# New ranks and engine allowances for all work from the second batch's keys on

## The chip, the cores and the metric

The kernel runs on one core of a Trainium2 chip. TensorE (PE; PEld is its weight load) does the matmuls, VectorE (DVE), ScalarE (ACT) and GpSimd (POOL) the elementwise work, and SyncE (SP) issues every DMA from one queue. Each engine works through its own instruction stream strictly in the order in which it was written and waits on semaphores of the others. The metric is the device time of one execution in microseconds, lower is better.

## The reference

Three layers over 4 batches of 576 tokens, in fp32:

```python
# attention: 8 heads of 64; heads 0-3 see the last 32 keys, heads 4-7 every 4th of the last 128
scores = np.where(mask, q @ k.T / 8, -1e9)
attn = np.exp(scores - max); attn = attn / (attn.sum() + 1e-9)
x = attn @ v                                    # (4, 576, 512)
# first feed-forward: x_prev is x shifted by one token
xk = mu_k * x + (1 - mu_k) * x_prev;  xr = mu_r * x + (1 - mu_r) * x_prev
k = np.maximum(xk @ w_k, 0);  v = k * k @ w_v   # w_k (512, 1024), w_v (1024, 512)
x = 1 / (1 + np.exp(-(xr @ w_r))) * v
# second: gated, with a mix over the tokens
h = np.maximum(x @ w_in, 0);  u, v = h[..., :512], h[..., 512:]
v_n = (v - mean(v)) / sqrt(var(v) + 1e-6)
v_s = einsum('ts,bsd->btd', w_spatial, v_n) + b_spatial[:, None]
out = (u * v_s) @ w_out
```

## The kernel before

**Numbers.** A product of two fp32 matrices is done as three matmuls in a faster type: each operand is split into a high part (a copy that rounds, on ACT or DVE) and a low part (a subtraction, on DVE or POOL). So every operand costs one copy and one subtraction before TensorE can read it. The function `halves` records both.

**Names.** Work is recorded in steps with a tag of step, batch and, where there are two, half: `ld` loads queries and keys (16 small DMAs for a half of the heads), `qk` turns them on DVE (tiles `qT`, `kT`), `vw` loads values (10 or 12 DMAs), `soft` is scores (`psS`), mask and maximum (`pr`, `mx`), exponential, sum and division (`sm`, `st`, `pr`), transposition on TensorE (`psT`) and copy (`pt`); `val` multiplies by the values and copies to `x`. `k` (mixed input `xd`, `xm`, `xh`, `xl`; after the matmul `kr`, then squares split into `kh`, `kl`, shown in profiles as `sq_dt`), `r` and `v` are the first feed-forward; `s` splits its successor's weights. In the second layer `x2`, `u2`, `v2`, `vn` do the input product by a seven-product scheme over 2 by 2 blocks; `V` splits the normalised half (tiles `V`, `VS`, `wt`), `sp` is the mix over tokens (sums in `R` or `wf`; the gated product is split into `gh`, `gl`), `out` the last product (`ot`, then the store).

**The order.** Nothing is issued while the steps are recorded. The class `Plan` keeps for each operation its dependencies, its engines with a cost in ns for each, and a base rank. At the end `Plan.order` plays a greedy schedule forward: whenever an engine is free, it takes, of the operations that are ready by the plan's own clock, the one with the lowest rank. If an operation may run on more than one engine, an engine takes it only when no other would end it sooner, each end counted with an allowance in ns that is added for DVE and POOL (ACT has none). The engines' instruction streams are then written in that order. The rank and the allowances come from the table `TUNE`; `k / count` runs from 0 to just under 1 over the operations of one kind in a step:

```python
more, grow, dve_, pool_ = TUNE.get(g[0], {}).get(g[1], (0, 0, 792, 22))
prio.append(o[5] + more + grow * (k / count[g]))
self.pens.append({"dve": dve_, "pool": pool_})
...
free[e] = start + (460 if e == "dma" else cost[e])
...
def dve(n):
    return 70 + n * 1.042
```

The base rank is about 1000 per half batch in the first layer (2825 and 3611 for the attention of batch 2), 10000 to 13500 in the second. Up to 100 us the plan also fills TensorE's idle time with matmuls on constants. Two tiles hold loaded queries and keys and two hold values, so a load can start only when its tile's last reader is done; the DMAs stand in SP's queue in the planned order, and one that waits holds up all behind it.

**Which order results.** Attention of a batch runs among the first feed-forward of the batch before it. The second layer begins near 320 us. Its last part, `V`, `sp` and `out` for the batches in the order 2, 3, 0, 1, begins near 455 us.

Of the kernel before, what the change touches and what calls it, by code (L numbers as in the profile page):

```python
# [36 lines left out]
def blocks(dil):  # L37
# [40 lines left out]
    ('out', 0): {'ot': (-48481, 1635, 400, -300), 'out': (-15787, -1962, 400, 2000), 'psB': (-26874, 3252, 200, 0)},  # L78
    ('out', 1): {'ot': (11033, 6529, 1500, 300), 'out': (81304, 27, 400, -800), 'psB': (60486, 11220, 1500, 2000)},
    ('out', 2): {'ot': (-40922, 4560, 792, -300), 'out': (29151, 33499, 200, -800), 'psB': (42562, 2655, 200, 22)},  # L80
    ('out', 3): {'ot': (-54092, -274, 200, 2000), 'out': (-39436, 37850, 200, -800), 'psB': (-39698, 3601, 200, 300)},
# [33 lines left out]
    ('spill', 0): {'spill': (-77802, 20888, 200, 2000)},  # L115
    ('spill', 1): {'spill': (7310, -4425, 1500, 800)},
    ('start',): {'ident': (5243, -7493, 792, 22), 'identb': (-2035, 973, 792, 22), 'mask': (0, 0, 792, 22), 'mask2': (0, 0, 792, 22), 'pt': (7412, 207, 792, 800), 'xok': (11235, 2251, 792, 22)},
    ('tail',): {'ed': (19937, 5909, -200, 800), 'eh': (19594, -4924, -600, 300), 'el': (26278, 3273, -200, 300), 'wt': (42392, -29077, 792, 2000)},
    ('tailu', 0): {'psB': (-49671, 13322, 1500, 0), 'utl': (-90359, -26564, 400, -800)},
# [2209 lines left out]
```

## Time and profile before

| | |
|---|---|
| median of 3 runs | 587.37 us (587.1 to 587.73) |
| the profiled execution's own time | 584.21 us |
| its span, first to last instruction | 582.4 us |
| PE busy | 556.1 us, 95% |
| DVE busy | 450.9 us, 77% |
| ACT busy | 300.4 us, 52% |
| POOL busy | 197.0 us, 34% |
| mean granted TensorE clock | 0.992 |

The profile is one execution; times inside it are counted from the span's start. Busy time of PE is the union of its matmuls, which are pipelined, so short stalls between them do not show as idle. The helper class that records the program gives nearly all instructions the same line, so they are told apart by their tiles.

### The profile page before, as it was taken

To read this page: it belongs to the slowest core of one execution; us is meant where nothing else is said; L and a number is where in the kernel's file an instruction comes from. 1 tells how busy PE (TensorE), PEld (TensorE's weight loads), DVE (VectorE), ACT (ScalarE), POOL (GpSimd) and SP (SyncE) were. 2 spreads that over 40 slices of the span, in tenths; PEclk is the share of its full clock that TensorE was granted. 3 is DMA by queue.
4 is the path that set the end of the run, shared out by engine and by line. 5 is a ranking of instruction groups with operands and counts; after the bars stand their busy time and mean duration, and the time that the engine had idled before them with its cause. 6 is when DMAs were issued, how large, how long until landed. Compare 5 with 4: busy or idle time off the path is not lost.

```text
span 582.4 us, 14108 instructions
## 1 busy us (share of the span) xinstructions
PE 556.1 (95%) x5714; PEld 517.8 (89%) x5715; DVE 450.9 (77%) x904; ACT 300.4 (52%) x734; POOL 197.0 (34%) x210
## 2 busy tenths in 40 slices
PE   8889999997989999999999999999999998899996
PEld 7767798796979999999999999999999998689885
DVE  7689998887979464554279984799989999976960
ACT  4579977785244271354738563364442466442231
POOL 1023402721144012122323501237664256573610
PEclk9899999999989999999999999999999999999999
DMA  9889572436656102000024120021010041311012
GB/s 243 243 204 217 146 187 48 77 95 129 105 129 121 19 29 65 1 2 1 1 73 146 52 62 1 26 59 73 1 74 2 1 181 36 109 73 55 2 73 91
DMA packets 91521, 47.35 MB, mean 81 GB/s; under 512 B 77184, under 2 KB 83328, under 8 KB 90944
## 3 DMA queue, kind: packets, MB, share of 16 engines
q1 hardware_dynamic: 91456, 46.45, 31.0%
q8 instruction: 45, 0.74, 0.5%
q14 instruction: 20, 0.16, 0.1%
HBM read 39.62 MB, written 6.82 MB: 80 GB/s over the span
## 4 chain that ended last, share of the span: by engine, by line
PE 66%; DVE 22%; ACT 5%; issue 3%; DMA 1%; POOL 1%; SPq 1%; DVEq 0%; ACTq 0%; POOLq 0%
PE psM L463 41%; PE psB L463 16%; PE psT L463 6%; DVE R L463 3%; PE psS L463 2%; DVE wf L463 2%; DVE num L463 2%; DVE x L463 1%; DVE V L463 1%; DVE VS L463 1%; DVE pt L463 1%; SPq L463 1%; DVE st L463 1%; DMA ld<-in_k_dram 1%; DVE X L463 1%
## 5 line engine op out<-in xcount | busy, mean ns | idle before, releaser
L463 PE MATMUL psM<-xh,wk 128*128 128x288 f32 x512 | 116.5, 325 | 2.2 <-ACT pr L463 1.1
L463 PE MATMUL psM<-sq_dt.float32r,wv 128*128 128x288 f32 x768 | 113.3, 298 | 0.0
L463 PEld LDWEIGHTS psM<-sq_dt.float32r,wv 128*128 128x128 f32 x768 | 104.9, 189 | 1.2
L463 PEld LDWEIGHTS psM<-xh,wk 128*128 128x128 f32 x512 | 87.2, 189 | 9.4 <-ACT pr L463 1.3
L463 PE MATMUL psM<-xh,wr 128*128 128x288 f32 x256 | 60.7, 300 | 0.4 <-ACT kr L463 0.2
L463 PE MATMUL psM<-xl,wk 128*128 128x288 f32 x192 | 56.6, 295 | 0.0
L463 POOL TENSOR_TENSOR xl<-xm,xh 128x288 fp32r<-128x288 f32 x26 | 25.0, 965 | 79.8 <-DVE xh L463 71.0
L463 PEld LDWEIGHTS psM<-xh,wr 128*128 128x128 f32 x256 | 44.0, 188 | 1.8 <-ACT kr L463 1.1
L463 PE MATMUL psM<-X,wu 128*128 128x256 f32 x336 | 42.8, 282 | 1.3 <-DVE x L463 1.3
L463 PE MATMUL psB<-wv,X 128*128 128x256 f32 x336 | 43.0, 283 | 0.2 <-DVE X L463 0.2
L463 PEld LDWEIGHTS psM<-X,wu 128*128 128x128 f32 x336 | 40.5, 188 | 2.0 <-DVE x L463 2.0
L463 PEld LDWEIGHTS psB<-wv,X 128*128 128x128 f32 x336 | 41.2, 190 | 0.5 <-DVE X L463 0.4
L463 PE MATMUL psB<-wo,gh 128*128 128x512 f32 x128 | 39.6, 391 | 0.0
L463 PE MATMUL psM<-xl,wr 128*128 128x288 f32 x128 | 37.9, 296 | 1.3 <-DVE xl L463 0.8
L463 POOL TENSOR_TENSOR pr<-pr,st 128x384 f32<-128x384 f32 (+1 forms) x22 | 20.0, 914 | 52.9 <-DVE st L463 48.9
L463 POOL TENSOR_TENSOR sq_dt.float32r<-kr,sq_dt.float32r 128x288 fp32r<-128x288 f32 x27 | 23.8, 883 | 36.9 <-DVE sq_dt.float32r L463 15.9
L463 PEld LDWEIGHTS psM<-xl,wk 128*128 128x128 f32 x192 | 36.2, 188 | 0.0
L463 ACT ACTIVATE kr<-psM 128x288 f32<-128x288 f32 x50 | 20.4, 408 | 29.9 <-PE psM L463 26.3
L463 DVE SCALAR_TENSOR_TENSOR xm<-xd,mu,x 128x288 f32<-128x288 f32 x56 | 31.9, 585 | 3.1 <-POOL xl L463 2.6
L463 ACT ACTIVATE x<-psM 128x288 f32<-128x288 f32 x32 | 12.9, 411 | 34.3 <-PE psM L463 34.2
L463 DVE TENSOR_TENSOR x<-psM,x 128x288 f32<-128x288 f32 x32 | 14.3, 451 | 20.0 <-PE psM L463 18.3
L463 ACT COPY pt<-psT 64x384 f32<-64x384 f32 (+1 forms) x34 | 16.6, 492 | 21.1 <-PE psT L463 14.5
(257 smaller groups left out, 1296.7 us busy)
## 6 DMA issues: line engine op xcount, KB each, us to landing
vw<-in_v_dram SPq DMA_DIRECT2D x36, 128.0 KB, 3.2
room<-in_moe_w_k_dram SPq DMA_DIRECT2D x8, 512.0 KB, 6.0
room<-in_moe_w_v_dram SPq DMA_DIRECT2D x8, 512.0 KB, 3.7
raw<-in_moe_w_in_dram SPq DMA_DIRECT2D x8, 512.0 KB, 4.0
out_dram<-ot SPq DMA_DIRECT2D x16, 256.0 KB, 2.0
ld<-in_k_dram SPq DMA_DIRECT2D x48, 72.0 KB, 3.3
ld<-in_q_dram SPq DMA_DIRECT2D x48, 72.0 KB, 2.5
vw<-in_v_dram SPq DMA_DIRECT2D x16, 144.0 KB, 4.8
```

The source lines that it names most:

```text
L463: return self.tc.keep_in_program_order(getattr(self.engine, name)(*args, **kw))
```

## The change

Only the table `TUNE` differs. All entries of batch 0, and of batch 1 those up to its attention, stay as they were; every entry from step `k` of batch 1 on has new numbers, ranks and allowances alike. No operation is added or taken out, and costs, dependencies and tiles are the same. The entries that the text speaks of (each is extra rank at the start, growth over the operations, DVE's allowance, POOL's allowance):

```diff
-    ('V', 1): {'V': (-5132, 2059, 0, -800), 'wt': (-431, 7469, 0, 800)},
-    ('V', 2): {'V': (-29642, 13773, 400, 2000), 'wt': (64135, 28781, 1500, -300)},
...
+    ('V', 1): {'V': (-49975, 24808, 792, 0), 'wt': (-44885, 22472, 1500, 0)},
+    ('V', 2): {'V': (-48767, 28868, 400, 2000), 'wt': (124793, 37230, -200, -800)},
...
-    ('k', 1, 0): {'kh': (-3048, -1140, 0, 22), 'kl': (335, -85, 200, 0), 'kr': (8547, -2346, -600, -300), 'psM': (-4354, 4007, 792, 22), 'xd': (4440, 7642, 1500, 22), 'xh': (-373, 12319, 0, 22), 'xl': (6520, 4617, 400, -300), 'xm': (-3560, 3912, 792, 22)},
-    ('k', 1, 1): {'kh': (-19369, -4576, -600, 22), 'kl': (227, 1222, 200, 22), 'kr': (-1162, -801, 200, 0), 'psM': (-4633, 3433, 792, 22), 'xd': (-4529, 8889, -600, -800), 'xh': (-1888, -4277, 400, 22), 'xl': (-2492, -6065, 200, 22), 'xm': (12647, 1915, 792, 22)},
...
+    ('k', 1, 0): {'kh': (62399, 23058, 1500, 2000), 'kl': (-68548, 9471, 1500, -300), 'kr': (-85236, -20357, 792, -800), 'psM': (-35217, 8418, 400, 800), 'xd': (56405, 11300, 1500, 0), 'xh': (-24180, 6644, -200, 22), 'xl': (-6277, 16030, -600, 0), 'xm': (-58090, -12486, 200, 300)},
+    ('k', 1, 1): {'kh': (-191685, -4254, 1500, 0), 'kl': (-107755, -4978, -600, 300), 'kr': (-33651, -4647, 792, 300), 'psM': (-32335, 24833, 200, 800), 'xd': (-36395, 15613, -600, 0), 'xh': (11222, 22389, 400, -800), 'xl': (-8229, 28500, 400, 0), 'xm': (2416, -21545, 400, 2000)},
...
-    ('ld', 2, 0): {'ld': (4613, 761, 792, 22)},
-    ('ld', 2, 1): {'ld': (-2722, 770, 792, 22)},
-    ('ld', 3, 0): {'ld': (14266, 7137, 792, 22)},
-    ('ld', 3, 1): {'ld': (130, -4585, 792, 22)},
+    ('ld', 2, 0): {'ld': (17759, 23620, 400, 22)},
+    ('ld', 2, 1): {'ld': (-58284, 15129, 0, 22)},
+    ('ld', 3, 0): {'ld': (-35119, 7865, -200, 300)},
+    ('ld', 3, 1): {'ld': (-56038, -4431, 0, 0)},
...
-    ('qk', 2, 0): {'kT': (-6562, -580, 792, 22), 'qT': (2754, 3285, 792, 22)},
-    ('qk', 2, 1): {'kT': (28122, 1894, 792, 22), 'qT': (9122, -1608, 792, 22)},
...
+    ('qk', 2, 0): {'kT': (-15538, -8809, 0, 22), 'qT': (7930, 24274, -200, 800)},
+    ('qk', 2, 1): {'kT': (88600, 15032, 1500, 2000), 'qT': (38625, 15852, 400, 2000)},
...
-    ('r', 1, 0): {'g': (10270, -8099, 792, 22), 'psM': (0, 0, 792, 22), 'xh': (-2437, -3689, 200, 22), 'xl': (7110, -8083, -600, 0), 'xm': (9866, -9493, 792, 22)},
...
+    ('r', 1, 0): {'g': (48897, -32478, 1500, 0), 'psM': (-14809, 17867, -200, -800), 'xh': (25859, -264, -600, 0), 'xl': (40031, -4652, 792, 22), 'xm': (59093, -26680, -200, 0)},
...
-    ('soft', 2, 0): {'mx': (-1247, 1522, 792, 22), 'pr': (-3600, -844, -200, 300), 'psS': (-9715, -5533, 792, 22), 'psT': (-14855, -4161, 792, 22), 'pt': (-8159, -7904, 200, 22), 'sm': (-3036, -2071, 792, 22)},
-    ('soft', 2, 1): {'mx': (9544, 1494, 792, 22), 'pr': (13284, -6468, 792, 22), 'psS': (-5404, 7060, 792, 22), 'psT': (-22380, -1749, 792, 22), 'pt': (628, -7502, 200, 22), 'sm': (-9958, 8076, 792, 22)},
...
-    ('sp', 0): {'R': (-14743, 15250, -600, 22), 'egh': (65748, 14140, 200, -300), 'egl': (26758, 12197, 792, 2000), 'gh': (-32947, -21591, 0, -800), 'gl': (-188971, -39155, 200, -800), 'psB': (63459, -38417, 1500, 800), 'psM': (5236, 16186, 792, 800)},
...
-    ('sp', 3): {'R': (14405, -2641, 0, 300), 'egh': (63114, -5793, 400, 2000), 'egl': (4229, 2868, 0, -800), 'gh': (-31376, -10686, 792, 22), 'gl': (-582, 12531, 1500, -300), 'psB': (-47640, -8795, 0, -800), 'psM': (-17530, 34434, 1500, 2000)},
...
+    ('soft', 2, 0): {'mx': (57838, 7572, 1500, -300), 'pr': (-15201, -24450, 1500, 300), 'psS': (-37032, -36836, 792, 0), 'psT': (-62504, -17366, 792, 0), 'pt': (-67780, -32544, 792, 300), 'sm': (-37940, -2255, 200, 300)},
+    ('soft', 2, 1): {'mx': (49556, 27536, -600, 300), 'pr': (73831, 15993, 400, -300), 'psS': (-16556, 14168, 792, -300), 'psT': (-81358, -3994, -600, 300), 'pt': (11200, -7427, 400, 22), 'sm': (-49384, 3395, -200, 0)},
...
+    ('sp', 0): {'R': (-56080, 8228, 0, 0), 'egh': (99232, 7166, -600, 2000), 'egl': (17995, 4130, -600, 2000), 'gh': (1849, -31309, 400, -800), 'gl': (-117458, -44454, -200, 2000), 'psB': (96057, -13044, 200, -300), 'psM': (1478, 427, 1500, 2000)},
...
+    ('sp', 3): {'R': (38469, -8591, 400, 22), 'egh': (49351, 12164, -200, 2000), 'egl': (-80398, 1446, 0, -300), 'gh': (-33594, -3462, -200, -300), 'gl': (4408, 3215, 0, 300), 'psB': (-19021, -2624, 1500, 300), 'psM': (44370, 38102, 200, 300)},
...
-    ('vw', 2, 0): {'vw': (-20808, -283, 792, 22)},
-    ('vw', 2, 1): {'vw': (-8875, -8535, 792, 22)},
-    ('vw', 3, 0): {'vw': (14126, -1721, 792, 22)},
-    ('vw', 3, 1): {'vw': (4271, 3636, 792, 22)},
...
+    ('vw', 2, 0): {'vw': (-59636, 10061, 792, -800)},
+    ('vw', 2, 1): {'vw': (-52395, 2167, 0, 300)},
+    ('vw', 3, 0): {'vw': (15050, 13464, -200, 300)},
+    ('vw', 3, 1): {'vw': (4463, -9688, -200, -300)},
...
```

## Rows read from the trace of the kernel before

**Rows 1.** The page, part 1: busy us and share of each engine.
```profile
PE 556.1 (95%) x5714; PEld 517.8 (89%) x5715; DVE 450.9 (77%) x904; ACT 300.4 (52%) x734; POOL 197.0 (34%) x210
```

**Rows 2.** Busy time by stretch: length, PE, PEld, DVE, ACT, POOL, PEclk, DMA share, GB/s.
```profile
0.00:100.00 100.00, 93.68 (x1399) 78.81 (x1401) 87.91 (x169) 73.33 (x222) 18.92 (x28) 0.98 0.77 185
...
125.00:175.00 50.00, 43.21 (x840) 39.99 (x828) 40.62 (x92) 22.68 (x56) 11.89 (x14) 0.97 0.60 120
175.00:300.00 125.00, 124.79 (x1205) 122.74 (x1202) 67.89 (x155) 55.50 (x121) 32.54 (x39) 1.00 0.15 34
300.00:322.00 22.00, 20.98 (x155) 20.31 (x154) 21.45 (x41) 15.84 (x34) 6.64 (x6) 1.00 0.32 108
...
385.00:410.00 25.00, 24.58 (x203) 23.69 (x202) 24.65 (x44) 13.21 (x29) 17.03 (x14) 1.00 0.13 50
...
455.00:515.00 60.00, 53.36 (x357) 48.78 (x356) 59.00 (x109) 31.27 (x67) 35.52 (x35) 1.00 0.24 84
```

**Rows 3.** PE's waits from 100 us on: total us, times, longest.
```profile
PE psT L463 <- DVE pr L463: 3.7, 2, 3.2
PE psM L463 <- DVE x L463: 2.3, 3, 1.1
PE psB L463 <- DVE R L463: 2.3, 3, 1.5
...
PE psT L463 <- POOL pr L463: 1.9, 1, 1.9
```

**Rows 4.** Timeline from 127 to 146 us: start, us, instruction, idle before and its releaser.
```profile
126.81 2.56 SPq L463 DMA_DIRECT2D vw<-in_v_dram  x4
...
129.46 3.38 SPq L463 DMA_DIRECT2D ld<-in_q_dram  x4
...
134.92 1.16 DVE L463 STREAM_TRANSPOSE qT<-ld 128x576 f32<-128x576 f32 x1 [3.59 <-DMA ld<-in_q_dram]
...
138.14 7.40 SPq L463 DMA_DIRECT2D vw<-in_v_dram  x10
...
138.62 0.52 PE L463 MATMUL psT<-ident,pr 128*128 128x128 f32 x3 [3.17 <-DVE pr L463]
```

**Rows 5.** The same from 158 to 172 us.
```profile
161.55 8.43 SPq L463 DMA_DIRECT2D vw<-in_v_dram  x12
...
164.49 0.40 PE L463 MATMUL psM<-xh,wk 128*128 128x288 f32 x1 [1.02 <-DVE x L463]
...
170.00 0.55 PE L463 MATMUL psT<-ident,pr 128*128 128x128 f32 x3 [1.85 <-POOL pr L463]
```

**Rows 6.** Busy time by stretch, one of 10 us.
```profile
170.00:180.00 10.00, 10.00 (x164) 9.36 (x165) 8.59 (x21) 6.71 (x17) 4.22 (x5) 0.83 0.79 152
```

**Rows 7.** Groups from 125 to 200 us on DVE: count, busy us, mean ns.
```profile
L463 DVE TENSOR_TENSOR xl<-xm,xh 128x288 fp32r<-128x288 f32 x8 | 3.5, 452 | 0.7 <-ACT xh L463 0.6
...
L463 DVE TENSOR_SCALAR kr<-psM 128x288 f32<-128x288 f32 x4 | 1.8, 446 | 0.0
L463 DVE CAST sq_dt.float32r<-kr 128x288 fp32r<-128x288 f32 x3 | 0.9, 302 | 0.4 <-ACT kr L463 0.3
```

**Rows 8.** Groups of the same stretch on ACT.
```profile
L463 ACT CAST sq_dt.float32r<-kr 128x288 fp32r<-128x288 f32 x6 | 2.6, 430 | 3.6 <-DVE kr L463 3.6
```

**Rows 9.** Groups from 455 to 515 us on DVE.
```profile
L463 DVE TENSOR_TENSOR VS<-wt,VS 128x512 fp32r<-128x512 f32 x9 | 8.8, 973 | 0.0
...
L463 DVE TENSOR_TENSOR wt<-num 128x512 f32<-128x512 f32 x2 | 2.0, 1017 | 0.0
```

**Rows 10.** Groups from 455 to 515 us on POOL.
```profile
L463 POOL TENSOR_TENSOR gl<-wf,gh 128x288 fp32r<-128x288 f32 (+1 forms) x7 | 7.8, 1126 | 5.9 <-ACT gh L463 5.9
L463 POOL TENSOR_TENSOR gl<-R,gh 128x288 fp32r<-128x288 f32 (+1 forms) x7 | 6.6, 949 | 3.2 <-ACT gh L463 3.1
```

**Rows 11.** Groups from 455 us to the end on DVE, where `gl` runs there.
```profile
L463 DVE TENSOR_TENSOR gl<-wf,gh 128x288 fp32r<-128x288 f32 (+1 forms) x4 | 1.7, 423 | 0.2 <-ACT gh L463 0.2
```

**Rows 12.** A group of the first 100 us on DVE, both operands in SBUF.
```profile
L463 DVE TENSOR_TENSOR wv<-temps,wv 128x512 fp32r<-128x512 f32 x8 | 5.3, 674 | 0.0
```

More of the change, by code (lines that the diff above doesn't have):

```diff
@@ L77 @@
     ('nat', 1): {'nat': (5726, -4074, 792, 22)},
[L78 to L81, printed above, removed]
[1 row of a table removed]
+    ('out', 0): {'ot': (-70225, 15926, 400, 0), 'out': (-30892, -23428, 792, 0), 'psB': (68651, 8775, 200, -300)},
+    ('out', 1): {'ot': (-71839, 10110, 1500, 0), 'out': (96695, 15148, 0, 0), 'psB': (194624, 3199, 792, 2000)},
+    ('out', 2): {'ot': (789, 1375, 400, -300), 'out': (29705, 63406, 0, 0), 'psB': (79999, 2399, -600, 800)},
+    ('out', 3): {'ot': (-125593, 3794, 1500, 22), 'out': (-27311, 59389, -200, -800), 'psB': (-121106, 49, 200, 800)},
[1 row of a table added]
     ('qk', 0, 0): {'nT': (3175, 2385, 792, 22)},
@@ L106 @@
     ('soft', 1, 1): {'mx': (-1252, 2068, 100, 22), 'pr': (223, 3165, 0, 2000), 'psS': (1897, 4328, 100, 22), 'psT': (-4852, -665, 100, 22), 'pt': (-12129, -6490, 400, 22), 'sm': (4162, -2435, 100, 22)},
[8 rows of a table removed]
-    ('spill', 0): {'spill': (-77802, 20888, 200, 2000)},
-    ('spill', 1): {'spill': (7310, -4425, 1500, 800)},
-    ('start',): {'ident': (5243, -7493, 792, 22), 'identb': (-2035, 973, 792, 22), 'mask': (0, 0, 792, 22), 'mask2': (0, 0, 792, 22), 'pt': (7412, 207, 792, 800), 'xok': (11235, 2251, 792, 22)},
-    ('tail',): {'ed': (19937, 5909, -200, 800), 'eh': (19594, -4924, -600, 300), 'el': (26278, 3273, -200, 300), 'wt': (42392, -29077, 792, 2000)},
-    ('tailu', 0): {'psB': (-49671, 13322, 1500, 0), 'utl': (-90359, -26564, 400, -800)},
-    ('tailu', 1): {'psB': (-24953, 17469, 1500, 300), 'utl': (-62624, -2995, 792, -800)},
-    ('tailv', 0): {'psB': (-27810, 8234, -600, 800), 'vtl': (40308, -4697, 1500, 300)},
-    ('tailv', 1): {'psB': (-76248, -1432, 1500, 22), 'vtl': (54592, -456, 0, 22)},
[4 rows of a table removed]
[8 rows of a table added]
+    ('spill', 0): {'spill': (-46337, 9059, 400, -300)},
+    ('spill', 1): {'spill': (-7782, -12257, -600, -300)},
+    ('start',): {'ident': (5243, -7493, 792, 22), 'identb': (-2035, 973, 792, 22), 'mask': (0, 0, 792, 22), 'mask2': (0, 0, 792, 22), 'pt': (7412, 207, 792, 800), 'xok': (11235, 2251, 792, 22)},
+    ('tail',): {'ed': (72061, -32525, 1500, 2000), 'eh': (11421, -4176, 792, 2000), 'el': (56661, 1588, -200, 800), 'wt': (38085, -32917, 200, 2000)},
+    ('tailu', 0): {'psB': (-92242, 7233, 200, 0), 'utl': (-89897, -12389, 1500, 0)},
+    ('tailu', 1): {'psB': (-115950, 45791, 1500, 22), 'utl': (-4650, -6543, 200, 2000)},
+    ('tailv', 0): {'psB': (-73183, 19252, 400, 2000), 'vtl': (2270, 8881, 0, 22)},
+    ('tailv', 1): {'psB': (-81478, 10506, 400, 0), 'vtl': (24309, -15136, -200, 22)},
[4 rows of a table added]
     ('v', 0, 0): {'g': (-13056, -4401, 792, 22), 'psM': (-8039, 2344, 792, 22)},
     ('v', 0, 1): {'g': (-810, -767, 792, 22), 'psM': (-2066, 2788, 792, 22)},
[10 rows of a table removed]
[10 rows of a table added]
     ('val', 0, 0): {'psT': (-5281, 5817, 792, 22), 'x': (-16083, -108, 400, 22)},
@@ L142 @@
     ('val', 1, 1): {'psT': (-7539, -7372, 792, 22), 'x': (-9000, 2119, 1500, 22)},
-    ('val', 2, 0): {'psT': (11217, 7583, 792, 22), 'x': (1769, -230, 200, 22)},
-    ('val', 2, 1): {'psT': (-2551, -876, 792, 22), 'x': (-10263, -5137, 0, 22)},
-    ('val', 3, 0): {'psT': (0, 0, 792, 22), 'x': (0, 0, 792, 22)},
-    ('val', 3, 1): {'psT': (-2074, 10315, 792, 22), 'x': (-194, -1787, -600, 22)},
[6 rows of a table removed]
+    ('val', 2, 0): {'psT': (65689, 6230, 0, 22), 'x': (115978, 7151, 792, 22)},
+    ('val', 2, 1): {'psT': (9256, -74, 400, 22), 'x': (-37554, -37012, 200, -300)},
+    ('val', 3, 0): {'psT': (5159, 837, -600, 22), 'x': (117728, -26283, 0, 0)},
+    ('val', 3, 1): {'psT': (20234, 2036, 400, 0), 'x': (-33851, 30630, 400, 2000)},
[6 rows of a table added]
     ('vs', 0, 0): {'vw': (11887, 5366, -600, 300)},
@@ L157 @@
     ('vw', 1, 1): {'vw': (14706, -1163, 792, 22)},
[6 rows of a table removed]
-    ('w', 'wiu'): {'low': (-12130, -17299, -600, -300), 'num': (72546, -39230, 1500, 800)},
-    ('w', 'wiu', 'ld'): {'raw2': (-41336, -1529, 792, 300)},
-    ('w', 'wiv'): {'low': (-67964, -20675, -600, -800), 'num': (47338, 10858, 792, 2000)},
[1 row of a table removed]
[6 rows of a table added]
+    ('w', 'wiu'): {'low': (-43972, -15505, -200, -800), 'num': (83432, -65770, 200, 2000)},
+    ('w', 'wiu', 'ld'): {'raw2': (-69565, 4722, -200, 0)},
+    ('w', 'wiv'): {'low': (13831, -21115, 0, 22), 'num': (92308, -16366, 200, 22)},
[1 row of a table added]
     ('w', 'wk'): {'low': (-878, 371, 792, 22), 'whole': (-5511, -123, 792, 22)},
     ('w', 'wk', 'ld'): {'raw': (226, 4234, 100, 22)},
[2 rows of a table removed]
[2 rows of a table added]
     ('w', 'wr'): {'low': (3812, -2292, 792, 22), 'part0': (1091, -5033, 400, 22), 'part1': (594, 903, 0, 0), 'tmp': (634, 1988, 100, 22)},
@@ L176 @@
     ('w2', 'wk'): {'part0': (17441, -4609, 200, 22), 'part1': (1157, -3153, 0, -300)},
[2 rows of a table removed]
-    ('wvroom',): {'wvroom': (13730, -1065, 792, 22)},
[4 rows of a table removed]
[2 rows of a table added]
+    ('wvroom',): {'wvroom': (0, 0, 792, 22)},
[4 rows of a table added]
 }
```

106 rows, old and new, of the table TUNE are left out of this document.

## The prediction

> **What bounds the kernel now.** The page's first part comes first: TensorE is busy for 556.1 of 582.4 us, so whatever a new order does, it can only win back TensorE's idle time, 26 us in all [rows 1]. As no operation is added, TensorE's own work stays the same. The second view is busy time by stretch. After the first 100 us, whose entries in the table stay, the idle time lies in two places: 6.8 us from 125 to 175 us and 6.6 us from 455 to 515 us, where DVE is busy for 59.0 of 60 us. From 300 to 322 and from 385 to 410 it is 1.0 and 0.4 us, with DVE full too; between 175 and 300 us it is 0.2 us [rows 2]. So some 15 us are within reach of the change. The third view, TensorE's waits, names who ended them: nearly always DVE, once POOL [rows 3].
>
> The fourth view, the timeline, shows how the first place comes about. SP sends value loads and then the next half's queries; DVE's transposition of these queries (`qT`) stands in DVE's stream before the softmax, so DVE sits idle for 3.59 us until the load lands, and what TensorE needs from the softmax behind it is late: TensorE idles for 3.17 us at 138.6 us [rows 4]. Two more stops follow, 1.02 us at 164.5 and 1.85 us at 170.0 us, again for work of DVE and of POOL [rows 5]. Behind them the granted clock of the next 10 us is 0.83, a mix of the two levels of 1.2 and 2.4 GHz, against 1.00 around it [rows 6]. That costs about 10 x 0.17 = 1.7 us of full speed, which TensorE's busy time hides.
>
> Why DVE runs late can be read from the code beside the rows. The plan counts 70 + 288 x 1.042 = 370 ns for a 288-wide DVE operation that takes 446 to 452 ns [rows 7], and 460 ns for a DMA where SP needs 2.56 / 4 = 640 to 7.40 / 10 = 740 ns for a value load [rows 4]. Where DVE is nearly full on the plan's clock, it overruns on the chip, and TensorE, whose order is fixed, waits.
>
> **The change, part by part.** The ranks and allowances say what is preferred; the resulting order is not in front of me, so I take from the table which way each group is pushed.
>
> *Loads and transpositions of batches 2 and 3.* The base ranks are 2353 to 4464 for `vw` and 2675 to 4786 for `ld`. The second half of batch 2's queries and keys gets -54800 to -40300 and its values -49300 to -46900, where before the values had -13200 to -5700 and went ahead of loads at 740 to 1800. For batch 3 the first half's values fall from some 17000 to 18700-31100, while its queries and keys rise to -31000 and above, and the second half's to -51600 and below. So when both could go, queries and keys now go first, and no longer stand behind 10 or 12 value loads that hold SP for 7.40 or 8.43 us [rows 4, 5]. Batch 2's second-half transpositions drop from some 9000 and 28000 to 38600 and 88600, so DVE does its other work first. Both push in one direction: the DVE wait of 3.59 us should shrink. Bounds: nothing comes back, if the transposition still stands ahead of a load in flight, or all 3.17 us of TensorE. The four value loads ahead of the queries at 129.5 us belong to batch 1, whose entries do not change, so the gain hangs on the transposition's place. I take 2.0 us. What is late next are the values of batch 2 (`vw`), 12 loads of 8.43 us; they are needed only for that batch's `x`, at the next half batch but one, so the 125 us in which TensorE loses 0.2 us cover them [rows 2, 5].
>
> *Copies and subtractions of batch 1.* In `k` of half 0, DVE's allowance goes from -600 to 792 for `kr`, from 0 to 1500 for `kh`, from 200 to 1500 for `kl`; in half 1 from -600 to 1500 for `kh`. All push work off DVE, to ACT and POOL. The 4 `xl` that `k` of half 0 pulls to DVE (400 to -600) are matched by 4 that `r` of half 0 sends away (-600 to 792). If half of the 8 + 8 `kr` operations of half 0 and the 3 casts of the stretch move, that is 8 x 0.446 + 3 x 0.302 = 4.5 us off DVE in 75 us [rows 7]. ACT takes a cast at 430 ns against DVE's 302 and is busy for only 22.68 of 50 us, so it has the room [rows 2, 8]. DVE full or late is what the stops at 164.5 and 170.0 us and the slow clock behind them come from, 1.02 + 1.85 + 1.7 = 4.6 us [rows 5, 6]; bounds 0 and 4.6, and I take 2.5, about half, because the last of the stops was released by POOL, which gets more work.
>
> *Softmax of batch 2.* Its maximum is put behind nearly everything (57838 and 49556 added), its transposition ahead of everything (-62504 and -81358). The maximum then waits for DVE's spare time, and TensorE takes the transposition the moment the plan thinks it ready. The first spreads DVE's load into 175 to 300 us, where DVE is busy for only 67.89 of 125 us [rows 2]; the second keeps the kind of wait that now costs 3.7 us [rows 3]. I count the two as nothing together; if the cover goes, it is a stop of 1 to 3 us as now.
>
> *The last part, 455 us on.* Here DVE is full, so each us put on it is nearly a us of TensorE. The `gl` subtractions of `sp` of batches 3 and 0 lose POOL's favour (1500 and -300 to 0 and 300; 200 and -800 to -200 and 2000): up to 16 go from POOL to DVE. About 12 would fall before 515 us, 12 x 0.423 = 5.1 us more on DVE [rows 11]. The 4 `wt` sums of `V` of batch 2 come half-way (1500 and -300 to -200 and -800). Against it, the `wt` sums of `V` of batch 1 go the other way (0 and 800 to 1500 and 0): up to 3 x 1.017 = 3.1 us off DVE [rows 9]. POOL is relieved of 12 x (7.8 + 6.6) / 14 = 12.3 us [rows 10]. DVE gains from that too: a 512-wide subtraction of two SBUF operands takes 973 ns here, beside a POOL busy for more than half of the time, and 674 ns early in the kernel [rows 2, 9, 12]. The Trainium skill's "GPSIMD Engine Reference", section 1 on specifications, says that GpSimd shares its SBUF interfaces with VectorE and contends with DVE instructions that have two SBUF inputs; the trace agrees by these 973 and 674 ns. Without the relief the sum here is 5.1 - 3.1 = +2.0 us. With it, if a third of those 12.3 us lay beside such operations, 12.3 / 3 x (1 - 674 / 973) = 1.3 us come back. I take +1.0; bounds -3.1 (sums of batch 1 leave, subtractions stay on POOL) and 16 x 0.423 + 4 x 1.017 = +10.8 (all 16 subtractions and batch 2's sums come, none leaves) [rows 9, 11].
>
> *All other entries* (batches 2 and 3 of the first feed-forward, the weights, `x2` to `vn`) act where TensorE is covered, except for 1.4 us at 300 and 385 us. I take 0, bounds -1.4 and +1.5.
>
> Sum: -2.0 - 2.5 + 1.0 = -3.5 us. The profiled execution took 584.21 us of its own time, 1.8 beyond its span, and would take 580.7; it is 3.2 us below the median of the three runs, so the forecast for the median is 587.37 - 3.5 = **583.9 us**.
>
> **The rivals.**
> *The last part overloads DVE (slower).* Its term comes out at the upper bound, +10.8 us, with the early gain of 4.5 as forecast: +6.3 us, 593.7. For it: DVE is busy for 59.0 of 60 us there and the allowances of `gl` and of batch 2's `wt` both turn to DVE [rows 2]; against it: those of batch 1's `wt` turn away, and 8 of the `gl` may come after 515 us, where it costs less. It decides from 4.5 us more of DVE work in that stretch, and shows as slower from 5.7.
> *The waits only move (same).* The order still trusts costs that are too low for DVE and SP, so TensorE meets as many stops elsewhere, within 1.2 us: 587.4. For it: the same plan made both orders; against it: the idle stretch from 175 to 300 us can take work.
> *Both places open up (much faster).* Early stops go wholly, 3.17 + 4.6 = 7.8 us, and the last part wins 3.1 by its sums and 1.4 by the quieter POOL, with 0.4 from the places between: 12.7 us, 574.7. For it: all terms are DVE's; against it: it needs every bound at its good end.
>
> **How the numbers follow.** What a measurement of this kernel can tell from no change is about 0.2%, 1.2 us. The likeliest, 583.9, has 0.44; its own range is 580.5 to 586.1. Much faster has 0.13, the waits only move 0.15, the overloaded last part 0.28. Faster is 0.44 + 0.13 = 0.57, same 0.15, slower 0.28. The range reaches to the good end of the bounds, 574.7, and short of the overloaded case's full price, to 593.0; beyond lie about half of that case's 0.28 and a little of the best, 2 in 10 or somewhat less.
>
> **What would show it.** Right: no DVE wait of over 1 us on `ld` near 130 us, PE above 46 of 50 us from 125 to 175 us, a clock of 1.00 behind it, `kr` and `sq_dt` casts on ACT, value loads behind the key loads, DVE still full in the last part with more `gl` on it. Wrong: TensorE stops at new places in 175 to 300 us, or loses over 8 us where the last part is full.

## The result, and the profile after

| | median | range | runs |
|---|---|---|---|
| before | 587.24 us | 586.75 to 587.73 | 4 |
| after | 581.15 us | 580.56 to 581.95 | 4 |

The ratio is 0.9897 with a 95% interval of 0.9880 to 0.9914: 6.05 us faster (5.0 to 7.0), where 3.5 were forecast. The profiled execution of after took 581.26 us of its own time with a span of 579.5, so profile against profile shows only 2.9 us. The other 3 us lie in the profiled execution of before, which was 3.0 us below the median (last section).

The page of after, part 1, answers to [rows 1]:

```profile
PE 558.8 (96%) x5715; PEld 518.2 (89%) x5715; DVE 445.0 (77%) x890; ACT 316.2 (55%) x768; POOL 193.4 (33%) x194
```

TensorE's idle time falls by 5.6 us, from 26.3 to 579.5 - 558.8 = 20.7 us; its busy time grows by 2.7, so the span shrinks by 2.9 only. Busy time by stretch, with the columns of [rows 2]; the last row, of 10 us, answers to [rows 6]:

```profile
125.00:175.00 50.00, 49.56 (x805) 47.26 (x804) 37.98 (x76) 32.37 (x71) 27.70 (x34) 1.00 0.60 101
175.00:300.00 125.00, 123.70 (x1297) 118.87 (x1296) 69.51 (x152) 66.70 (x151) 17.25 (x21) 1.00 0.18 45
455.00:515.00 60.00, 54.89 (x350) 49.25 (x349) 59.91 (x118) 29.36 (x61) 34.99 (x32) 1.00 0.25 93
170.00:180.00 10.00, 10.00 (x139) 9.91 (x129) 7.96 (x18) 3.49 (x7) 4.58 (x5) 1.00 0.62 99
```

From 125 to 175 us TensorE is busy for 49.56 us where it was 43.21, DVE loses 2.64 us, ACT gains 9.69 and POOL 15.81, and the clock behind it is 1.00 instead of 0.83. From 175 to 300 us TensorE loses 1.30 us instead of 0.21. Together that is 5.3 us less idle time, nearly all of the 5.6. In the last part it is busy for 54.89 instead of 53.36, with DVE full as before. Its waits from 100 us on, as in [rows 3]:

```profile
PE psM L463 <- DVE wf L463: 4.1, 5, 1.2
PE psM L463 <- DVE x L463: 1.4, 2, 1.1
```

The waits on `pr`, 3.7 and 1.9 us before, are gone; those on `wf`, behind 480 us, have grown from 2.1 us. The timeline of the place of [rows 4]:

```profile
131.60 3.22 SPq L463 DMA_DIRECT2D ld<-in_q_dram  x4
...
136.97 1.21 DVE L463 STREAM_TRANSPOSE qT<-ld 128x576 f32<-128x576 f32 x1 [0.39 <-DMA ld<-in_q_dram]
137.08 7.11 SPq L463 DMA_DIRECT2D vw<-in_v_dram  x10
...
138.89 8.18 PE L463 MATMUL psM<-sq_dt.float32r,wv 128*128 128x288 f32 x60
```

and DVE alone, later:

```profile
156.00 0.78 DVE L463 STREAM_TRANSPOSE qT<-ld 128x576 f32<-128x576 f32 x1 [3.20 <-DMA ld<-in_q_dram]
159.27 0.78 DVE L463 STREAM_TRANSPOSE kT<-ld 128x576 f32<-128x576 f32 x1 [2.50 <-DMA ld<-in_k_dram]
```

DVE has other work until the queries have landed and idles for 0.39 us, and TensorE runs 60 matmuls on end. Ten value loads still stand ahead of further queries, but the next twelve, the values of batch 2's second half, which went out from 161.55 us on [rows 5], now follow all queries and keys of batch 3:

```profile
178.00 2.06 SPq L463 DMA_DIRECT2D ld<-in_q_dram  x4
180.16 35.39 SPq L463 DMA_DIRECT2D vw<-in_v_dram  x16
```

DVE still waits for loads, 3.20 and 2.50 us, but TensorE then holds the product of step `k` for the next half, whose inputs are all there: it runs from 148.04 us on without a stop and starts the scores that need these loads only at 160.85 us. Before, the next scores came at 152.61 us. TensorE's rows, of after and then of before:

```profile
160.85 1.10 PE L463 MATMUL psS<-kT,qT 64*32 64x64 f32 x64
```

```profile
152.61 1.77 PE L463 MATMUL psS<-kT,qT 64*32 64x64 f32 x112
```

Groups of 125 to 200 us in after, to set against [rows 7, 8]:

```profile
L463 POOL TENSOR_TENSOR sq_dt.float32r<-kr,sq_dt.float32r 128x288 fp32r<-128x288 f32 x8 | 6.7, 860 | 0.0
...
L463 ACT ACTIVATE kr<-psM 128x288 f32<-128x288 f32 x13 | 5.3, 411 | 9.6 <-PE psM L463 8.7 <-POOL sq_dt.float32r L463 0.7
L463 ACT CAST sq_dt.float32r<-kr 128x288 fp32r<-128x288 f32 x12 | 5.1, 430 | 1.5 <-POOL kr L463 0.9 <-PE psM L463 0.5
...
L463 DVE TENSOR_TENSOR xl<-xm,xh 128x288 fp32r<-128x288 f32 x6 | 3.8, 629 | 0.1
```

All 4 `kr` and all 3 casts have left DVE. The last part in after, 455 to 515 us, to set against [rows 9, 10]:

```profile
L463 DVE TENSOR_TENSOR VS<-wt,VS 128x512 fp32r<-128x512 f32 x10 | 10.0, 999 | 0.0
...
L463 POOL TENSOR_TENSOR V<-num,V 128x512 fp32r<-128x512 f32 x2 | 4.7, 2372 | 0.0
...
L463 POOL TENSOR_TENSOR gl<-wf,gh 128x288 fp32r<-128x288 f32 (+1 forms) x4 | 4.2, 1042 | 2.9 <-DVE wo L463 2.0 <-ACT gh L463 0.9
...
L463 POOL TENSOR_TENSOR gl<-R,gh 128x288 fp32r<-128x288 f32 (+1 forms) x4 | 3.8, 970 | 3.1 <-ACT gh L463 3.1
...
L463 DVE TENSOR_TENSOR gl<-R,gh 128x288 fp32r<-128x288 f32 (+1 forms) x4 | 2.7, 687 | 0.0
...
L463 DVE TENSOR_TENSOR gl<-wf,gh 128x288 fp32r<-128x288 f32 (+1 forms) x4 | 2.5, 630 | 0.0
```

Eight `gl` run on DVE where there were none, and POOL, relieved of 6 of its 14, does `V` sums instead. One and the same matmul near the start of that part, in before and then in after:

```profile
463.83 3.12 PE L463 MATMUL psM<-X,wu 128*128 128x256 f32 x24 [1.08 <-DVE x L463]
```

```profile
461.09 3.11 PE L463 MATMUL psM<-X,wu 128*128 128x256 f32 x24 [1.08 <-DVE x L463]
```

It stands 2.74 us earlier in after; the spans differ by 2.9. So in these two executions the last part gives 0.2 us, and the gain is made ahead of it.

### The profile page after: what moved, and what is told of

The parts are those of the page before. It is cut to its first block, busy times and chain, and to the rows that moved or that the text cites. A ratio compares the mean times of both kernels' runs of the same rounds, so it can differ in the third digit from the quotient of the medians.

```text
span 579.5 us, 14116 instructions
## 1 busy us (share of the span) xinstructions
PE 558.8 (96%) x5715; PEld 518.2 (89%) x5715; DVE 445.0 (77%) x890; ACT 316.2 (55%) x768; POOL 193.4 (33%) x194
## 4 chain that ended last, share of the span: by engine, by line
PE 72%; DVE 14%; ACT 7%; POOL 4%; issue 3%; ACTq 0%; DVEq 0%; POOLq 0%
PE psM L463 46%; PE psB L463 16%; PE psT L463 7%; PE psS L463 3%; DVE wf L463 2%; DVE R L463 2%; ACT pr L463 2%; ACT kr L463 1%; POOL wsT L463 1%; DVE VS L463 1%; DVE V L463 1%; ACT pt L463 1%; DVE num L463 1%; DVE x L463 1%; ACT L463 1%
## 5 line engine op out<-in xcount | busy, mean ns | idle before, releaser
L463 ACT ACTIVATE kr<-psM 128x288 f32<-128x288 f32 x59 | 24.0, 407 | 27.5 <-PE psM L463 25.8
L463 ACT CAST xh<-xm 128x288 fp32r<-128x288 f32 x40 | 17.1, 433 | 25.8 <-PE psM L463 17.4
L463 POOL TENSOR_TENSOR xl<-xm,xh 128x288 fp32r<-128x288 f32 x19 | 17.7, 942 | 38.5 <-ACT xh L463 25.5
L463 DVE TENSOR_TENSOR sq_dt.float32r<-kr,sq_dt.float32r 128x288 fp32r<-128x288 f32 x38 | 20.8, 548 | 11.9 <-ACT sq_dt.float32r L463 11.6
L463 PE MATMUL psT<-const-bfloat16-1.0 128*128 128x224 bf16 x224 | 27.8, 278 | 1.3 <-PEq L2312 0.8
```

The lines of the kernel that those rows point to most:

```text
L463: return self.tc.keep_in_program_order(getattr(self.engine, name)(*args, **kw))
```

## The experiments

Three kinds, each timed against before on its own chip (before was between 587.59 and 588.58 us in these). "New" and "old" stand for the tables after and before.

| run | what is new | median | ratio to before, 95% |
|---|---|---|---|
| e1_first | table entries of the first layer | 602.96 us | 1.0263 (1.0229 to 1.0298) |
| e2_second | table entries of the second layer | 609.30 | 1.0370 (1.0330 to 1.0409) |
| e9_soft | table entries `soft`, `val` of batches 2, 3 | 620.00 | 1.0543 (1.0514 to 1.0572) |
| e5_allow | allowances of `k`, `r` of batch 1 | 591.08 | 1.0051 (1.0027 to 1.0074) |
| h1_first_all | first layer, place and engine | 584.87 | 0.9956 (0.9937 to 0.9975) |
| h2_second_all | second layer, place and engine | 592.21 | 1.0070 (1.0045 to 1.0094) |
| h3_first_order | first layer, place alone | 591.44 | 1.0068 (1.0045 to 1.0091) |
| h4_first_engine | first layer, engine alone | 594.34 | 1.0120 (1.0095 to 1.0145) |
| h5_last | all but the last part | 581.80 | 0.9904 (0.9881 to 0.9928) |
| h6_att | attention, place and engine | 596.70 | 1.0164 (1.0140 to 1.0188) |
| h7_ffn | first feed-forward, place and engine | 603.92 | 1.0285 (1.0263 to 1.0308) |
| q1_turn | one transposition moved | 587.14 | 0.9986 (0.9965 to 1.0007) |

**Parts of the table.** A part of the entries is new and the whole is planned anew. e1_first takes those of the first layer, e2_second all others, e9_soft the eight of `soft` and `val` of batches 2 and 3, e5_allow only the allowances of four entries:

```diff
 e1_first, one of 38 entries
-    ('ld', 2, 1): {'ld': (-2722, 770, 792, 22)},
+    ('ld', 2, 1): {'ld': (-58284, 15129, 0, 22)},
 e2_second, one of 53 entries
-    ('V', 1): {'V': (-5132, 2059, 0, -800), 'wt': (-431, 7469, 0, 800)},
+    ('V', 1): {'V': (-49975, 24808, 792, 0), 'wt': (-44885, 22472, 1500, 0)},
 e9_soft, one of 8 entries
-    ('val', 2, 0): {'psT': (11217, 7583, 792, 22), 'x': (1769, -230, 200, 22)},
+    ('val', 2, 0): {'psT': (65689, 6230, 0, 22), 'x': (115978, 7151, 792, 22)},
 e5_allow, one of 4 entries
-    ('r', 1, 0): {'g': (10270, -8099, 792, 22), 'psM': (0, 0, 792, 22), 'xh': (-2437, -3689, 200, 22), 'xl': (7110, -8083, -600, 0), 'xm': (9866, -9493, 792, 22)},
+    ('r', 1, 0): {'g': (10270, -8099, 1500, 0), 'psM': (0, 0, -200, -800), 'xh': (-2437, -3689, -600, 0), 'xl': (7110, -8083, 792, 22), 'xm': (9866, -9493, -200, 0)},
```

> The table of before with all new entries of the first layer (steps k, r, v, soft, val, qk, ld, vw); the second layer keeps its old entries. Theory 1 (the gain comes from the early place, 125 to 175 us): the whole gain or nearly, 5 to 6 us below before, about 581.5 to 582.5, PE above 49 of 50 us from 125 to 175 us. Theory 2 (it comes from the last part): no more than 1.2 us below before, 586 or above. Half and half: 584.

> The table of before with all new entries of the second layer (weights, x2 to vn, V, sp, out); the first layer keeps its old entries and so its three stops between 138 and 172 us. Theory 1: within 1.2 us of before, 586 to 588.5, PE still near 43 of 50 us from 125 to 175 us. Theory 2: 4 to 6 us below before, about 582, with PE above 55 of 60 us from 455 to 515 us. By the prediction's term for the last part alone: 1 us above before.

> The table of before with only the new entries of soft and val of batches 2 and 3. DVE then does other softmax work ahead of the transposition of the queries that waits for its load. If the softmax ranks are what takes the stop of 3.17 us away (the prediction counted them as nothing): 2 to 4 us below before, no wait of TensorE on pr over 1 us near 138 us. If, as the prediction has it, loads and transpositions do that: within 1.2 us of before.

> The ranks of before throughout; only the engine allowances of steps k and r of batch 1 (4 entries) are the new ones, so that copies and subtractions leave DVE for ACT and POOL. The prediction's term: 2.5 us below before (bounds 0 to 4.6), DVE busy for less than 40 of 50 us from 125 to 175 us. Rival: the place of loads, transpositions and softmax in the order makes the gain, and this is within 1.2 us of before.

All four are slower, by 3.0 us (e5_allow) to 32 us (e9_soft); no theory had that. Windows of e1_first:

```profile
125.00:175.00 50.00, 49.55 (x804) 47.26 (x804) 38.17 (x77) 32.52 (x71) 27.45 (x34) 1.00 0.57 103
175.00:300.00 125.00, 123.77 (x1298) 118.98 (x1297) 69.47 (x152) 66.48 (x151) 17.42 (x21) 1.00 0.18 45
...
410.00:455.00 45.00, 41.20 (x331) 40.39 (x330) 41.18 (x79) 16.84 (x34) 19.96 (x16) 0.96 0.06 25
455.00:515.00 60.00, 51.66 (x328) 45.56 (x327) 50.87 (x98) 27.39 (x58) 21.58 (x22) 0.89 0.18 62
```

Up to 300 us this kernel is as good as after, 49.55 and 123.77 us of TensorE in the two stretches. It loses behind that, where its entries are the old ones: 41.20 of 45 us from 410 to 455 us, where before has no idle time, and 51.66 of 60 with a clock of 0.89 from 455 on. So a part of the table cannot be timed by itself: the greedy planner, starting the second layer from another state, makes another order there too. The allowances alone, e5_allow, give +3.0 us (1.6 to 4.4) where the prediction had -2.5. Its trace shows what relief of DVE is worth by itself. From 125 to 175 us DVE is busy for 33.15 us, as expected below 40. It still idles for 4.20 us at 136.54 us, until the queries have landed, and TensorE stops for 3.52 us at 141.48 us: it is busy for 43.41 us, where before has 43.21, and the clock is 0.93.

**Joined orders.** So both tables are planned, and each operation keeps the place in time and the engine that one of the plans gives it; dependencies stay ahead of what needs them. All else is left as it was, but an operation can be pushed back by what it depends on. For h1_first_all:

```diff
-        _, self.out = self.schedule(self.tuned())
+        _, other = self.schedule(self.tuned(OTHER))
+        _, own = self.schedule(self.tuned())
+        seat = {i: (t, e) for t, i, e in own}
+        for t, i, e in other:
+            tag = self.tags[i]
+            if tag[0] in ("k", "r", "v", "soft", "val", "qk", "ld", "vw"):
+                seat[i] = (t, e)
...
+        while ready:
+            t, i = min(ready)
+            ready.remove((t, i))
+            self.out.append((t, i, seat[i][1]))
...
```

h2_second_all has `if not (tag[0] in (...))`, h3_first_order `seat[i] = (t, seat[i][1])`, h4_first_engine `seat[i] = (seat[i][0], e)`.

> Both orders are planned, with the old and the new table, and then joined: the operations of the first layer (k, r, v, soft, val, qk, ld, vw) stand in the place and on the engine that the new table gives them, all others in the place and on the engine of the old table. Theory 1 (the gain is made in the first layer, and the mixed tables lost because the planner goes astray with ranks that were not set together): 3 to 6 us below before, 581.5 to 584.5, and the last part as before. Theory 2 (the two halves need each other on the chip as well): 5 us or more above before, as with the mixed tables. Theory 3 (the gain comes from the second layer): within 1.2 us.

> The counterpart: operations of the second layer in the place and on the engine of the new table, those of the first layer as before. Theory 1: within 1.2 us of before, the three stops between 138 and 172 us still there. Theory 2: 5 us or more above before. Theory 3: 3 to 6 us below before. The prediction's term for the last part: 1 us above before.

> Joined in the same way, but the operations of the first layer take only their place in time from the new table; their engines are the old ones. If the order of loads, transpositions and softmax makes the gain of the first layer: at least two thirds of the gain of the run with both, 2 to 4 us below before. If the shift of copies and subtractions from DVE to ACT and POOL makes it: less than a third of that gain, or slower, since DVE is then late where the new order counts on the other engines. The prediction's split: 2.0 of 4.5 us from the order.

> The opposite half: the operations of the first layer keep their old place in time and take only their engine from the new table. TensorE's and SP's streams are then those of before. By the prediction 2.5 us below before (bounds 0 to 4.6), by the relief of DVE; the stop of 3.17 us behind the queries' load stays, as the loads stand where they stood. If the order makes the gain: within 1.2 us of before, or slower, as ACT and POOL take longer for the same work.

The first layer alone gives -2.6 us (-3.7 to -1.5). That is short of theory 1's 3 to 6 us, with an interval that reaches into it; theories 2 and 3 are out. Its windows show the gain of after up to 300 us (from 175 us on TensorE is busy for 123.76 of 125 us), and a loss where the old second layer begins, 1.54 us from 322 to 385 us where before has none:

```profile
125.00:175.00 50.00, 49.56 (x813) 47.21 (x810) 38.07 (x76) 32.99 (x73) 27.24 (x33) 1.00 0.58 104
...
322.00:385.00 63.00, 61.46 (x471) 60.45 (x471) 44.50 (x82) 29.32 (x65) 12.30 (x11) 1.00 0.15 43
```

The second layer alone is 4.1 us slower (2.6 to 5.5), between what theories 1 and 2 had. Here too the place where the layers meet is dear; TensorE's longest wait is there:

```profile
315.16 0.41 PE L580 MATMUL psM<-xh,wk 128*128 128x288 f32 x1 [3.31 <-DVE x L580]
```

Place alone and engine alone are both slower, +4.0 us (2.6 to 5.3) and +7.0 us (5.6 to 8.5), while both together are 2.6 us faster. With the new places and the old engines, TensorE stops for DVE again, for `pr` (0.84 us at 139 us) and for a `kr` that the new table has off DVE:

```profile
157.59 0.40 PE L580 MATMUL psM<-xh,wk 128*128 128x288 f32 x1 [1.22 <-DVE kr L580]
```

With the new engines and the old places the stop behind the queries' load remains under another name: DVE's copy `pt` stands behind the transposition that waits for the load, ACT's next copy waits for that one, and TensorE for ACT:

```profile
136.62 1.16 DVE L580 STREAM_TRANSPOSE qT<-ld 128x576 f32<-128x576 f32 x1 [3.55 <-DMA ld<-in_q_dram]
...
137.81 0.56 DVE L580 COPY pt<-psT 64x384 f32<-64x384 f32 x1
...
138.41 0.47 ACT L580 COPY pt<-psT 64x384 f32<-64x384 f32 x1 [2.96 <-DVE pt L580]
...
138.93 0.80 PE L580 MATMUL psT<-pt,vw 128*64 128x64 f32 x20 [1.95 <-ACT pt L580]
```

**Smaller steps.** q1_turn takes before's order and moves one transposition by 3.7 us of the plan's time; nine rows of DVE's stream change, and no other stream does. h5_last is after with the last part as before. h6_att and h7_ffn split the first layer in two.

```diff
 q1_turn
+        for i, o in enumerate(ops):
+            if self.tags[i] == ("qk", 2, 1) and o[6][0] == ("qT", 0, 0):
+                seat[i] = (seat[i][0] + 3700, seat[i][1])
 h5_last, with the new table as own and the old one as other
+            if tag[0] in ("V", "sp", "out"):
+                seat[i] = (t, e)
 h6_att
+            if tag[0] in ("soft", "val", "qk", "ld", "vw"):
 h7_ffn
+            if tag[0] in ("k", "r", "v"):
```

> The order of before with one operation moved: the first transposition of batch 2's second half of queries, for which DVE idles 3.59 us until the load lands, stands some eight places later in DVE's stream, behind the softmax work that TensorE waits for. All other streams are those of before. The prediction's term for loads and transpositions: 2.0 us below before (bounds 0 and 3.17), no wait of TensorE on pr of over 1 us near 138 us. Rival: the stop comes back at the next work that DVE owes, or in the loads queued behind the tile that the transposition frees later; then within 1.2 us of before.

> The order of after, with the operations of the last part (V, sp, out) in the place and on the engine of the old table. If the last part's new entries are worth nothing, as the busy times of the two profiles say: within 1.2 us of after, about 581, so some 6 us below before. If the 3.7 us by which after stands below the run with only the first layer new come from the last part: 584 to 585. By the prediction's term (new last part 1 us dearer): 580. By its rival of the overloaded last part: 571.

> The order of before, with the attention of batches 1 to 3 (soft, val, qk, ld, vw) in the place and on the engine of the new table; k, r and v stay. If attention's order and engines alone make the gain: 2 to 4 us below before. If, as the runs with order and engines apart suggest, the two layers of the change need each other: 0 to 4 us above before, because DVE still holds the copies that the new order wants off it.

> The counterpart: the first feed-forward (k, r, v) in the place and on the engine of the new table, attention as before. By the prediction's term for copies and subtractions: 2.5 us below before (bounds 0 and 4.6), with the stop of 3.17 us near 138 us still there. If the parts need each other: 0 to 5 us above before.

q1_turn is 0.8 us faster with an interval from 2.1 us faster to 0.4 slower: no difference that shows. Its trace says why. One DVE copy ahead of the edit, in before and in q1_turn:

```profile
124.62 0.42 DVE L463 COPY x<-psT 128x256 f32<-128x256 f32 x1 [1.50 <-PE psT L463]
```

```profile
127.90 0.43 DVE L482 COPY x<-psT 128x256 f32<-128x256 f32 x1 [1.50 <-PE psT L482]
```

This execution is 3.28 us behind there, from causes ahead of the edit. The rest, from the timelines of SP and then of TensorE in q1_turn:

```profile
132.99 3.25 SPq L482 DMA_DIRECT2D ld<-in_q_dram  x4
...
164.97 9.00 SPq L482 DMA_DIRECT2D vw<-in_v_dram  x12
```

```profile
138.67 0.55 PE L482 MATMUL psT<-ident,pr 128*128 128x128 f32 x3
...
155.07 1.75 PE L482 MATMUL psS<-kT,qT 64*32 64x64 f32 x108 [1.47 <-DVE kT L482]
...
158.09 0.41 PE L482 MATMUL psM<-xh,wk 128*128 128x288 f32 x1 [0.68 <-DVE kr L482]
...
174.35 1.45 PE L482 MATMUL psT<-pt,vw 128*64 128x64 f32 x40 [0.62 <-DMA vw<-in_v_dram]
177.08 0.80 PE L482 MATMUL psT<-pt,vw 128*64 128x64 f32 x20 [1.28 <-DMA vw<-in_v_dram]
...
181.44 0.40 PE L482 MATMUL psM<-xh,wr 128*128 128x288 f32 x1 [0.84 <-DVE kr L482]
```

The last of these matmuls in before:

```profile
177.69 0.30 PE L463 MATMUL psM<-xh,wr 128*128 128x288 f32 x1
```

The matmul that stopped for 3.17 us at 138.62 us [rows 4] starts at 138.67, 0.05 us behind: the stop is gone. The loads did not move with it: they still go out 3.5 us behind those of before (queries at 132.99 against 129.46 us [rows 4], values at 164.97 against 161.55 [rows 5]). TensorE, now early, meets them: 1.47 us for `kT`, then 0.62 and 1.28 us for the value loads that the prediction held to be covered, 3.4 us against the 3.2 won. DVE is late as well: 0.68 and 0.84 us for `kr`, and 1.12 us for `pr` where before has 0.51; in return the stop of 1.02 us for `x` [rows 5] is gone. With the wait on POOL, 1.85 us before and 1.71 now, TensorE's stops from 138 us to the last matmul shown add up to 6.6 us in before and 7.7 us in q1_turn. That matmul is 3.75 us behind, where the distance was 3.28 ahead of the edit. So the rival of its expectation holds: the next loads, and work that DVE then owes, take the gain back.

h5_last is as fast as after: by the ratios 0.9904 and 0.9897 the new last part gives 0.4 us, with an interval from 2.1 us faster to 1.3 slower, so no effect of it shows. Where h1_first_all lost 1.54 us behind the first layer, it loses next to nothing:

```profile
322.00:385.00 63.00, 62.94 (x494) 62.67 (x493) 44.90 (x78) 31.14 (x70) 18.09 (x15) 1.00 0.16 46
```

h6_att and h7_ffn are slower by 9.6 us (8.2 to 11.0) and 16.7 us (15.5 to 18.1), far more than expected, and together they make the gain of h1_first_all. In h6_att TensorE's longest stop from 135 to 195 us is for a transposition, in h7_ffn for the softmax at the old place. These stops are a small part of the losses: from 175 to 300 us, where before has 0.21 us of idle time, TensorE idles for 4.26 us in h6_att and 4.68 in h7_ffn, and the rest was not traced.

```profile
171.12 0.86 PE L580 MATMUL psS<-kT,qT 64*32 64x64 f32 x44 [2.20 <-DVE qT L580]
```

```profile
141.29 0.52 PE L580 MATMUL psT<-ident,pr 128*128 128x128 f32 x3 [2.64 <-DVE pr L580]
```

## Why the prediction came out right, and where its steps did not hold

The place was right: in after, 5.3 of the 5.6 us by which TensorE's idle time falls lie from 125 to 300 us, around the stops near 140 and 170 us. Each sign named for it appeared (DVE's wait on `ld` 0.39 us, PE 49.56 of 50 us, clock 1.00, `kr` and casts off DVE, twelve of the value loads behind the keys), and no stop of over 1 us came from 175 to 300 us. The sum behind the forecast did not hold, and that it came into its range is in part luck: its two gains, tried one by one, came out as no difference and as losses, and in the split by runs at the end of this section half of the gain stands where the sum had 0.

*Loads and transpositions, -2.0 us.* The stop went as described. But "the 125 us in which TensorE loses 0.2 us cover them", said of the values of batch 2, failed: q1_turn, which does this step alone, takes the stop away and meets `kT` and the values within 40 us. In after 12 of the 22 loads of these values go out behind the keys, and TensorE fills the time with a product that is ready. That this grouping is what lets the early start last is read from the traces; it was not tried by itself.

*Copies and subtractions, -2.5 us.* The operations moved as said, and DVE is busy for 54.88 instead of 61.26 us from 125 to 200 us. By itself the move costs 3.0 us (e5_allow, planned anew) or 7.0 (h4_first_engine, all engines of the first layer, old places): a DVE with less to do still waits for the queries' load, 4.20 us in e5_allow and 3.55 in h4_first_engine. The step that failed is the sum: it adds the two terms, and they do not add. Place +4.0 and engine +7.0 make -2.6 together, attention +9.6 and feed-forward +16.7 make the same -2.6. The size of their sum, -4.5, stands between h1_first_all's -2.6 (-3.7 to -1.5) and h5_last's -5.6 (-7.0 to -4.2). The slow clock, 1.7 us of this term, is gone in after; no run has its worth by itself.

*Softmax of batch 2, 0.* Not separated: e9_soft was planned anew and lost 32 us all over, h6_att holds it together with the loads.

*The last part, +1.0 us.* No effect shows: -0.2 us by the two marks, and -0.4 (-2.1 to 1.3) by h5_last, an interval that still holds the +1.0. The term's parts came out otherwise than priced. Eight `gl` came to DVE, not 12, and took 687 and 630 ns, not 423: 5.2 us, near the 5.1 forecast. POOL was not relieved (34.99 against 35.52 us), as it took two `V` sums, 4.7 us together, so `VS` stayed slow, 999 ns against 973. The `wt` sums did not leave: two `wt<-num` run on DVE as before, in 680 ns each instead of 1017. What made room on DVE are those `V` sums (4 instead of 6 run there) and sums `R` and `num`. The rival of the overloaded last part (593.7) is out. Of the others, "the waits only move" fits q1_turn but not the whole change, and of "both places open up" the early place did and the last part did not.

*All other entries, 0 (-1.4 to +1.5).* This term was too small. Between h1_first_all and h5_last lies only the second layer ahead of its last part, and 0.0052 of the time, 3.1 us (1.3 to 4.8, the two intervals taken as independent). Its entries are worth this where they follow the new first layer; e1_first shows what the old ones can cost there.

In all, taking the new parts in the order first layer, rest, last part: -2.6 where the prediction had -4.5, -3.1 for 0, -0.4 for +1.0. As differences of runs they make up the 6.05 us measured. They hold for this order alone: with the second layer first, its step is +4.1 (h2_second_all) and the first layer's -10.2. In after's own trace TensorE idles for 1.3 us from 300 to 455 us, in before's for 1.4. This reads as if the new entries there keep the gain of the first layer rather than make one of their own; no run separates the two.

A price that the prediction drew on shows once more: DVE's `xl`, two SBUF operands, takes 629 ns in the mean here against 452 [rows 7], with POOL busy for 29.72 of 75 us instead of 19.79. The mean mixes two kinds. Four of the six take 0.45 or 0.46 us, as before, while POOL is idle; the others take 0.90 us at 159.97 and 1.05 us at 164.35 us, beside subtractions of POOL (`sq_dt`, 158.98 to 160.56 and 163.09 to 165.09 us). The Trainium skill's "GPSIMD Engine Reference", section 1 on specifications, says that GpSimd shares its SBUF interfaces with VectorE and contends with DVE instructions that have two SBUF inputs, and the trace agrees by these 0.45 and 0.90 to 1.05 us.

## What to carry to other kernels

Taking one stop away from a pipeline is worth only the distance to the next thing that is late: look for that in the trace (here the next loads, by time of issue) before the stop is booked as a gain. Relief for an engine does not help where that engine waits for something else. Who does the work and when it is done is one decision where engines stand near full: each half of the new first layer was worse than the old one, by place and engine as by kind of work. To time a part of an order made by a greedy planner, join the finished orders instead of mixing its inputs, look at the places where the parts meet, and say which part went first.

## What was not expected of the hardware

Executions of the same instructions differ by some 2 us in the first 70 us. ACT's table load at the end of that stretch, in before, after and q1_turn, which have the same stream up to there:

```profile
70.38 1.28 ACT L463 ACT_TABLE_LOAD   x1
```

```profile
72.43 1.28 ACT L463 ACT_TABLE_LOAD   x1
```

```profile
72.75 1.28 ACT L482 ACT_TABLE_LOAD   x1
```

Before's profiled execution was early by 2.05 and 2.37 us, which is most of the 3.0 us by which it undercut the median. The one of h5_last, which comes to this load at 70.37 us, undercut its own by 2.5 us. A part of the difference shows in TensorE's first 79 matmuls, on a constant: 9.28 us in before, 10.48 in after, 9.74 in q1_turn. What makes the stretch vary stays open.

The prediction read 446 ns of a 288-wide DVE operation as its cost, against the plan's 370. Records of operations back to back overlap:

```profile
143.09 0.45 DVE L463 TENSOR_TENSOR x<-psM,x 128x288 f32<-128x288 f32 x1
143.46 0.94 DVE L463 SCALAR_TENSOR_TENSOR xm<-xd,mu,x 128x288 f32<-128x288 f32 x2
```

The first lasts 0.45 us, but the next starts 0.37 us behind it. So the plan's 370 ns was right for an operation like this, and "why DVE runs late" in the prediction does not hold for DVE's costs where POOL does not disturb it; it holds for SP's loads, of which 10 take 7.11 us in after, 711 ns each against the plan's 460.
